# Whole-head rounds in a two-cache decode attention kernel: 64 KB runs, a three-part key ring and one value slot

## The chip, the cores and the metric

One core of one Trainium2 chip. The metric is the device time of one execution in microseconds (us); several executions of each kernel are timed and the median is quoted. The "span" of a profile is the time from the first to the last instruction of one profiled execution. The kernel before takes 1335.8 us.

## The reference

Two attention layers decode one token each. Layer A has 32 heads, each with its own cache of 32,768 keys and values of 128 bf16 numbers (8 MB of keys and 8 MB of values for a head). Layer B has 8 key/value heads for 32 query heads and looks only at the last 4096 positions. In shortened form:

```python
def _A_ref(x, k_cache, v_cache, wq, wo):           # B has rep = 4 and a window of 4096 keys
    q = (x @ wq).reshape(B, Sq, H, Dh).transpose(0, 2, 1, 3)
    scores = jnp.einsum("bhqd,bhkd->bhqk", q, k_cache) * (Dh ** -0.5)
    p = softmax(scores, axis=-1)
    o = jnp.einsum("bhqk,bhkd->bhqd", p, v_cache)
    return o.transpose(0, 2, 1, 3).reshape(B, Sq, H * Dh) @ wo
return jnp.concatenate([a, b], axis=-1)
```

Every key and value is read once: 570.43 MB in all. Nearly all of it is A's cache.

## The kernel before

The program is a list of operations on each engine; dependencies become semaphore waits. DMA requests are made by SP (SyncE), in one order, and wait there until their buffer is free. Keys lie in two buffers of 32 KB per partition, values in two more. A round is half the keys of two heads: two 4 MB pieces of keys (one of each head), two of values. Shortened:

```python
def load_kv(self, which, name, g, r, u):           # one 4 MB piece: 32 KB runs on 128 partitions
    ...
    src = d[which][0, h0:h0 + d["kvu"], base:base + d["blk"], :].rearrange("s (p j) d -> p s (j d)", p=128)
    self.load_slot(which, slot, dst, src)          # waits until this slot is free

for i in range(self.NIT):                          # the main loop, 32 rounds
    g, r = divmod(i, a["R"])
    self.emit_qcopy(g)
    for u in range(2):
        self.load_kv("k", "A", g, r, u)
        self.emit_unit("A", g, r, u)               # T: transpose keys on PE, copy on DVE; S: scores
    self.emit_stats("A", g, r)                     # maximum and exp, running over r
    self.emit_PT("A", g, r)                        # transpose the probabilities
    for u in range(2):
        self.load_kv("v", "A", g, r, u)
        self.emit_PV("A", g, r, u)                 # 128 matmuls of 128 columns for each u
    self.emit_gather("A", g, r)
```

In what follows T is the transposes of the keys (PE into `psT`, DVE copies to `kt`), S the scores into `psS`, PV the product with the values into `psACC`, gather the small matmul into `psG`. Each operation signals one other engine. PV signals DVE, so SP learns that a value buffer is free from the next PE operation, the gather.

## Time and profile before

| | before |
|---|---|
| time, median (range) | 1335.74 us (1335.54 to 1335.80) |
| bytes read, mean rate | 570.43 MB, 428 GB/s |
| one round | 38.86 us for 16.8 MB, 431.8 GB/s |
| PE busy | 956.5 us, 72% |

The page of the kernel before: span, moved GB/s in 40 equal slices, packets, and the chain of waits that ended last (share of the span by line).

```profile
span 1334.2 us, 41413 instructions
...
PE 956.5 (72%) x19416; PEld 771.4 (58%) x19416; DVE 790.9 (59%) x1662; ACT 61.2 (5%) x201; POOL 2.0 (0%) x15
...
GB/s 393 394 424 436 427 435 428 434 430 432 431 433 431 432 431 430 433 431 432 431 432 430 432 433 430 433 431 433 428 434 429 432 432 432 432 430 434 430 433 351
DMA packets 22003, 570.64 MB, mean 428 GB/s; under 512 B 2530, under 2 KB 2532, under 8 KB 2788
...
DMA kbuf<-in_A_k_cache_dram 63%; PE psT L469 23%; PE psS L492 4%; DMA kbuf<-in_A_wo_dram 2%; PE psPT L634 0%; DVE out_sb L638 0%; SPq L291 0%
```

From the ninth slice on the rate is level at 428 to 434 GB/s, but for the last slice. The Trainium skill, "DMA: Bandwidth & Descriptors", section "Where 436 GB/s comes from", gives 435.2 GB/s as the ceiling of the 16 ports through which the DMA engines reach SBUF (the core's own memory), and a lower one, about 358, for loads from HBM (the main memory); this trace goes past the lower one and its level part sits about 1% under 435.2. The DMA queue is the bottleneck, so a question about time is a question about bytes per us and about empty moments.

One round in the timeline of the kernel before (start, length, engine, line, operation; in brackets the idle time ahead of it and what ended it):

```profile
659.86 5.37 PE L469 MATMUL psT<-ident,kbuf 128*128 128x128 bf16 x64 [4.02 <-DMA kbuf<-in_A_k_cache_dram]
...
670.49 10.08 SPq L291 DMA_DIRECT2D kbuf<-in_A_k_cache_dram  x2
...
686.97 3.58 PE L562 MATMUL psACC<-vbuf,ptsb 128*2 128x128 bf16 x128 [0.69 <-ACT ptsb L540]
...
691.09 1.96 PE L562 MATMUL psACC<-vbuf,ptsb 128*2 128x128 bf16 x128 [0.53 <-DVE oc_A L591]
...
693.66 0.44 PE L605 MATMUL psG<-oc_A,hw 128*32 128x1 f32 x4 [0.62 <-DVE oc_A L591]
693.89 0.81 SPq L291 DMA_DIRECT2D vbuf<-in_A_v_cache_dram  x2
```

The next round's T starts at 698.73, 38.87 us later, again after a wait for keys. T starts when the first 4 MB piece has landed, so at 693.89, where the values are asked for, the second piece is still ahead of them in the queue. That is 4.8 us to the landing plus 9.7 us for the second piece.

Four stretches of the table of windows of the kernel before. Columns: stretch, length, busy us of PE, PEld, DVE, ACT and POOL with counts, then the granted clock of PE, the DMA share and GB/s.

```profile
687.00:690.50 3.50, 3.50 (x128) 3.27 (x128) 0.00 (x0) 0.14 (x2) 0.00 (x0) 0.50 1.00 431
691.10:693.10 2.00, 1.94 (x128) 1.75 (x128) 0.00 (x0) 0.00 (x0) 0.00 (x0) 1.00 0.99 426
40.00:44.00 4.00, 3.42 (x40) 2.75 (x44) 4.00 (x7) 1.05 (x4) 0.00 (x0) 0.76 0.85 354
52.00:56.00 4.00, 4.00 (x63) 1.83 (x64) 1.51 (x6) 0.00 (x0) 0.00 (x0) 0.57 0.43 135
```

A hole is a time in which DMA engines have nothing to move.

### The profile page before, as it was taken

What the parts mean: (1) busy time and instruction counts of PE and PEld (TensorE: products, weight loads), DVE (VectorE), ACT (ScalarE), POOL (GpSimd) and SP (SyncE); (2) the same over time, 40 slices, a digit from 0 to 9 for tenths busy, and PEclk for the clock granted to TensorE, in tenths of its full rate; (3) what the DMA queues carried; (4) which work ended last, traced back from release to release, by engine and by line L of the source; (5) the groups of instructions that cost most, each with busy time, mean ns of one, the idle gap of its engine ahead of it and who ended that gap; (6) DMA issues with size and microseconds to landing.
All of it is one profiled execution on the core that took longest, in us unless ns stands there. A gap on an engine that the chain in (4) does not pass through costs nothing.

```text
span 1334.2 us, 41413 instructions
## 1 busy us (share of the span) xinstructions
PE 956.5 (72%) x19416; PEld 771.4 (58%) x19416; DVE 790.9 (59%) x1662; ACT 61.2 (5%) x201; POOL 2.0 (0%) x15
## 2 busy tenths in 40 slices
PE   3677667877767677776668777667777767677776
PEld 3456555656655565665556556555666655566663
DVE  3665555666555566655556665556666555566752
ACT  0000000000000000000000000000000000000000
POOL 0000000000000000000000000000000000000000
PEclk9787878888878888887888898878888878888988
DMA  9999999999999999999999999999999999999998
GB/s 393 394 424 436 427 435 428 434 430 432 431 433 431 432 431 430 433 431 432 431 432 430 432 433 430 433 431 433 428 434 429 432 432 432 432 430 434 430 433 351
DMA packets 22003, 570.64 MB, mean 428 GB/s; under 512 B 2530, under 2 KB 2532, under 8 KB 2788
## 3 DMA queue, kind: packets, MB, share of 16 engines
q1 hardware_dynamic: 21700, 570.44, 99.6%
q8 instruction: 10, 0.16, 0.0%
q10 hardware_dynamic: 288, 0.00, 0.0%
q14 instruction: 5, 0.04, 0.0%
HBM read 570.43 MB, written 0.00 MB: 428 GB/s over the span
## 4 chain that ended last, share of the span: by engine, by line
DMA 65%; PE 26%; issue 0%; DVE 0%; SPq 0%
DMA kbuf<-in_A_k_cache_dram 63%; PE psT L469 23%; PE psS L492 4%; DMA kbuf<-in_A_wo_dram 2%; PE psPT L634 0%; DVE out_sb L638 0%; SPq L291 0%
## 5 line engine op out<-in xcount | busy, mean ns | idle before, releaser
L472 DVE COPY kt<-psT 128x1024 bf16<-128x1024 bf16 x1056 | 655.1, 684 | 214.0 <-PE psT L469 211.6
L469 PE MATMUL psT<-ident,kbuf 128*128 128x128 bf16 x8448 | 576.0, 233 | 139.8 <-DMA kbuf<-in_A_k_cache_dram 129.7
L469 PEld LDWEIGHTS psT<-ident,kbuf 128*128 128x128 bf16 x8448 | 536.0, 106 | 232.8 <-DMA kbuf<-in_A_k_cache_dram 137.8
L562 PE MATMUL psACC<-vbuf,ptsb 128*2 128x128 bf16 (+1 forms) x8256 | 188.4, 271 | 45.4 <-ACT ptsb L540 22.0
L562 PEld LDWEIGHTS psACC<-vbuf,ptsb 128*2 128x2 bf16 (+1 forms) x8256 | 169.2, 106 | 66.8 <-ACT ptsb L540 30.5
L492 PE MATMUL psS<-kt,qw 128*32 128x512 bf16 x2048 | 157.7, 385 | 15.2 <-DVE kt L472 15.2
L537 PE MATMUL psPT<-ident,psb 128*128 128x128 bf16 x136 | 20.7, 307 | 130.9 <-ACT psb L524 130.9
L591 DVE SCALAR_TENSOR_TENSOR oc_A<-psACC,hot_A,oc_A 128x128 f32<-128x128 f32 x48 | 16.8, 351 | 145.5 <-PE psACC L562 145.5
L537 PEld LDWEIGHTS psPT<-ident,psb 128*128 128x128 bf16 x136 | 11.8, 131 | 140.7 <-ACT psb L524 140.3
L524 ACT ACTIVATE psb<-psS,nb_A 128x512 bf16<-128x512 f32 x32 | 22.0, 688 | 1173.9 <-DVE nb_A L523 1173.9
L492 PEld LDWEIGHTS psS<-kt,qw 128*32 128x32 bf16 x2048 | 33.9, 95 | 57.7 <-DVE kt L472 31.0
L588 DVE TENSOR_SCALAR oc_A<-psACC,hot_A 128x128 f32<-128x128 f32 x16 | 5.6, 350 | 92.8 <-PE psACC L562 92.8
L510 DVE TENSOR_REDUCE tr_in<-psS 128x1 f32<-128x512 f32 x34 | 23.5, 692 | 18.4 <-PE psS L492 18.4
L605 PE MATMUL psG<-oc_A,hw 128*32 128x128 f32 (+1 forms) x128 | 14.4, 223 | 23.8 <-DVE oc_A L591 19.4
L513 DVE COPY m<-tr_a 1x16 f32<-1x16 f32 (+1 forms) x136 | 22.3, 164 | 2.6
L605 PEld LDWEIGHTS psG<-oc_A,hw 128*32 128x32 f32 x128 | 6.6, 110 | 28.8 <-issue 28.8
L519 DVE COPY b_A<-mr_A 1x16 f32<-1x16 f32 x128 | 21.2, 165 | 2.4
L540 ACT ACTIVATE ptsb<-psPT 128x512 bf16<-128x512 bf16 x34 | 20.3, 597 | 21.3 <-PE psPT L537 21.3
L574 DVE TENSOR_SCALAR oc_A<-oc_A,alpha_A 128x129 f32<-128x129 f32 x16 | 4.6, 289 | 16.5 <-ACT alpha_A L527 16.5
L426 PE MATMUL psACC<-x_B,vbuf 128*128 128x1 bf16 x128 | 3.6, 165 | 13.5 <-DMA vbuf<-in_B_wq_dram 13.5
L426 PEld LDWEIGHTS psACC<-x_B,vbuf 128*128 128x128 bf16 x128 | 3.5, 104 | 13.4 <-issue 13.4
L527 ACT ACTIVATE alpha_A<-cm_A,nb_A 128x1 f32<-128x1 f32 x32 | 9.0, 282 | 0.0
(71 smaller groups left out, 107.6 us busy)
## 6 DMA issues: line engine op xcount, KB each, us to landing
kbuf<-in_A_k_cache_dram SPq DMA_DIRECT2D x64, 4096.0 KB, 28.2
vbuf<-in_A_v_cache_dram SPq DMA_DIRECT2D x64, 4096.0 KB, 30.6
kbuf<-in_B_k_cache_dram SPq DMA_DIRECT2D x2, 4096.0 KB, 27.8
vbuf<-in_B_v_cache_dram SPq DMA_DIRECT2D x2, 4096.0 KB, 18.6
vbuf<-in_B_wq_dram SPq DMA_DIRECT2D x1, 4096.0 KB, 12.6
vbuf<-in_A_wq_dram SPq DMA_DIRECT2D x1, 4096.0 KB, 41.8
kbuf<-in_B_wo_dram SPq DMA_DIRECT2D x2, 2048.0 KB, 25.9
kbuf<-in_A_wo_dram SPq DMA_DIRECT2D x1, 1536.0 KB, 22.5
```

Source lines behind the costliest of these rows:

```text
L469: inst = e.transpose(T[:, 128 * k:128 * k + 128], src[:, DH * tile:DH * tile + DH], self.ident[:, :])
L472: self.copies.append(self.op("dve", lambda v: v.tensor_copy(KT[:, :], T[:, :]), o, to="pe"))
L492: inst = e.matmul(self.S[32 * c:32 * c + 32, :], lhsT=win, rhs=self.kt[(bb + c // 2) % NKT][:, 512 * (c % 2):512 * (c % 2) + 512], start=f ...
L510: o = dve(lambda v: v.reduce_max(tr["in"][:, 0:1], self.S[:, :], axis=AXX), self.sdone, self.k_pool)
L513: x = dve(lambda v, c=c: v.tensor_copy(m4[0:1, W * c:W * c + W], tr["a"][32 * c:32 * c + 1, 0:W]), o)
L519: x = dve(lambda v, c=c: v.tensor_copy(t["b"][32 * c:32 * c + 1, 0:W].rearrange("p (k h) -> p k h", k=KC), t["mr"][0:1, k, :].unsqueeze(1) ...
L524: self.sread = self.op("act", lambda s: s.activation(out=self.psb[:, :], in_=self.S[:, :], func=ACTF.Exp, bias=t["nb"][:, k:k + 1], scale= ...
L537: inst = e.transpose(PT[:, 128 * jj:128 * jj + 128], self.psb[:, 128 * jj:128 * jj + 128], self.ident[:, :])
L540: self.ptread = self.op("act", lambda s: s.activation(out=self.ptsb[:, :], in_=PT[:, 0:512], func=ACTF.Copy), self.psread, to="pe")
L562: inst = e.matmul(acc[32 * c:32 * c + HG, 0:w], lhsT=pt[:, col:col + HG], rhs=vv[:, :, 16 * kc + 4 * c + jj, :], start=(kc == 0 and jj == ...
L591: self.oop = dve(lambda v, src=src, hot=hot: v.scalar_tensor_tensor(out=oc, in0=src, scalar=hot, in1=oc, op0=ALU.mult, op1=ALU.add), pv, b ...
L605: self.gath = self.op("pe", lambda e, c=c, c2=c2: e.matmul(self.G[0:32, c0 + c:c0 + c2], lhsT=win, rhs=t["oc"][:, c:c2], start=False, stop ...
```

## The change

A round becomes one whole head. Its 8 MB of keys are one transfer with 64 KB runs per partition into two neighbouring thirds of a 96 KB ring, its 8 MB of values one transfer into a single 64 KB slot. There is then no running maximum and no rescaling, and PV uses 64 matmuls of 512 columns. The intent is fewer, longer runs and less compute. The middle third is used by every head and transposed first, so that the next head's keys can be asked for half way through T. The last head's keys still come in two pieces. The startup is reordered as well.

```diff
-        self.kbuf = [sb(f"kbuf{i}", [128, UT * DH], BF16) for i in range(2)]
-        self.vbuf = [sb(f"vbuf{i}", [128, UT * DH], BF16) for i in range(2)]
+        self.kbuf = sb("kbuf", [128, 3 * HALF * DH], BF16)
+        self.vbuf = sb("vbuf", [128, 2 * HALF * DH], BF16)
 ...
+    def k_thirds(self, g):
+        return (1, 0) if g % 2 == 0 else (1, 2)
+    def load_k(self, g, parts):
 ...
+        if parts == 1:
+            self.load(self.kbuf[:, w * lo:w * lo + 2 * w], src, self.mark("k", 0), *free)
+            sem = self.mark("k", 1)
+            self.op("sp", lambda e: e.sem_inc(sem, 16))
+        else:
+            for i, t in enumerate(self.k_thirds(g)):
+                self.load(self.kbuf[:, w * t:w * t + w], src[:, w * (t - lo):w * (t - lo) + w], self.mark("k", i), *free)
+    def load_v(self, g):
+        self.load(self.vbuf[:, :], self.kv_src("v", "A", g)[:, 0, :], self.mark("v", 0), *self.free["v"])
 ...
         self.load_wq("B")
-        for g in range(2):
-            self.load_kv("k", "B", g, 0, 0)
+        self.load_b("k", 0)
         self.load_wq("A")
+        self.load_b("k", 1)
         self.emit_qproj("B")
-        self.emit_unit("B", 0, 0, 0)
+        self.emit_unit("B", 0)
+        self.emit_qproj("A")
 ...
-        for i in range(self.NIT):
-            g, r = divmod(i, a["R"])
-            self.loop = {"pe": i, "dve": g}
+        for g in range(NQH):
+            self.loop = {"pe": g // 2, "dve": g // 2}
+            self.load_k(g, 1 if g < NQH - 1 else 2)
+            self.load_v(g)
 ...
+            todo = [(c, pt[:, :, 32 * c + kc], self.vbuf[:, DH * (16 * kc + 4 * c):DH * (16 * kc + 4 * c + 4)], kc == 0, kc == 15)
+                    for kc in range(16) for c in range(STRIPS)]
 ...
+        pv = self.op("pe", mm, self.landed("v", 0 if name == "A" else g), self.ptread, self.accread, to="dve")
+        for i in (0, 1) if name == "A" else (g,):
+            self.free["v"][i] = pv
```

## The prediction

> **What bounds it now.** Data transfers. The page's slices show DMA at 9 tenths throughout, 430 to 434 GB/s in most; queue q1 holds 99.6%. In the timeline a round (half the keys of two heads, 16.8 MB) repeats every 38.86 us: 431.8 GB/s. PE works about 28 us of it (table of windows) and waits 129.7 us in all for keys (list of waits), so PE has slack; the chain of waits is 63% key loads. The Trainium skill, "DMA: Bandwidth & Descriptors", section "Where 436 GB/s comes from", puts the ceiling at 435.2 GB/s; the trace agrees, no long stretch is above it. The page's 570.43 MB at that rate is an estimated 1311 us, 1.9% below today: over 2% is practically out of reach.
>
> **What the change does.**
> 1. Runs double. In the trace's packet records 32 KB take 1.214 to 1.218 us, 16 KB 0.611 to 0.615, 8 KB 0.309 to 0.316, 4 KB 0.160: a line with 9 to 13 ns fixed per packet. If a 64 KB run is one packet, head loads need 512 fewer on each engine: 5 to 6 us saved (estimate from these); a round becomes about 38.7 us.
> 2. Startup. Before, one value load and A's first keys are issued only at 53.7 us (timeline); DMA is at 0.85 in 40 to 44 us and 0.43 in 52 to 56 (table of windows), about 2.8 us lost. Now A's projection runs earlier, the second value half is asked for near 40 us: 2.5 to 3 us gained.
> 3. Compute. PV becomes 64 matmuls of 512 columns instead of 256 of 128; rescaling, running maximum and alpha go. PV took 6.1 us with its gap (timeline); I expect 4. Off the critical path.
> 4. Queue depth. Next keys go out when the middle third is transposed, 10.6 us into the round, while values (19.4 us) are moving. Values go out at the gather, about 32.8 us in, 6 us before the keys in flight land. A transfer takes about 2.5 us to start (the hole at 53.7), so the queue should stay full, with 3.5 us to spare instead of about 12.
> 5. Tail. The last values land as one 8 MB piece; the last PV starts about 2 us later, and the end comes about 1 us later.
>
> Sum: -5.5 - 2.7 + 1 = about -7 us.
>
> **Prediction: 1328.7 us**, 8 in 10 between 1323.5 and 1335. Chances: faster by over 2% 0.02, within 2% 0.95, slower by over 2% 0.03.
>
> **What would show the steps right or wrong.** About 14,000 packets rather than 22,003, the 64 KB ones taking 2.42 us (1; if packets stay at 32 KB, only 2 us are gained in all). DMA share near 1 between 40 and 60 us (2). PE busy down by some 60 us (3). Value issues 5 to 6 us before keys land, steady slices at 432 to 434 GB/s (4). The last PV about 29 us after the last head's first keys (5).
>
> **What would make it wrong.** Value slot freed too late under a low granted clock: a hole of 1 to 2 us each round, +30 to +60 us. PE's loop over two heads is about 1560 instructions (780 matmuls, each with its weight load) against 1170; the skill's "Runtime: NRT & Kernel Launch", section "Instruction fetch mechanics", gives PE room for 2048, in blocks of 256. Today instruction fetches stop after the first rounds; if the longer loop refetches, stalls like the 4.5 us one at 110 us recur and use up the spare of step 4. 64 KB runs could stream slower from memory than 32 KB ones; nothing in this trace shows it.

## The result

The changed kernel takes 1341.97 us (1340.55 to 1344.51, 4 runs) beside 1335.77 (1335.54 to 1336.15) for the kernel before. Ratios are computed as the mean time of one kernel's runs over that of the other's of the same rounds, so they are not quite the ratio of the medians: here 1.0048, 95% interval 1.0031 to 1.0066. I had predicted a gain of 7 us with a range of 1323.5 to 1335; it lost 6.

The page of the changed kernel:

```profile
span 1340.9 us, 28815 instructions
...
PE 960.0 (72%) x13272; PEld 667.2 (50%) x13272; DVE 804.6 (60%) x1660; ACT 54.8 (4%) x167; POOL 2.0 (0%) x15
...
GB/s 395 442 427 428 422 426 438 432 420 428 436 409 438 438 409 438 438 434 432 416 436 434 411 438 426 420 438 438 432 428 422 438 438 438 438 432 420 427 439 284
DMA packets 12932, 570.66 MB, mean 426 GB/s; under 512 B 1522, under 2 KB 1524, under 8 KB 1780
```

Many slices read 438 and others 409, but slices cannot be read so finely here: a slice is 33.5 us long and a packet is booked whole at its start, so 14 packets of 64 KB on each of 16 engines make 438 GB/s and 13 make 407. What the page does show is the mean, 426 against 428, and a last slice of 284 against 351. PE busy has not fallen.

A round in the timeline of the changed kernel, and the end of the next one:

```profile
670.18 5.57 PE L485 MATMUL psT<-ident,kbuf 128*128 128x128 bf16 x64 [3.05 <-DMA kbuf<-in_A_k_cache_dram]
...
681.00 0.33 SPq L283 DMA_DIRECT2D kbuf<-in_A_k_cache_dram  x1
...
697.31 5.60 PE L573 MATMUL psACC<-vbuf,ptsb 128*4 128x512 bf16 x64 [0.69 <-ACT ptsb L548]
...
704.62 0.44 PE L599 MATMUL psG<-oc_A,hw 128*32 128x1 f32 x4 [1.72 <-DVE oc_A L587]
704.85 0.33 SPq L283 DMA_DIRECT2D vbuf<-in_A_v_cache_dram  x1
...
709.71 6.25 PE L485 MATMUL psT<-ident,kbuf 128*128 128x128 bf16 x64 [4.65 <-DMA kbuf<-in_A_k_cache_dram]
...
737.51 5.97 PE L573 MATMUL psACC<-vbuf,ptsb 128*4 128x512 bf16 x64 [0.69 <-ACT ptsb L548]
...
745.42 0.33 SPq L283 DMA_DIRECT2D vbuf<-in_A_v_cache_dram  x1
...
748.41 5.70 PE L485 MATMUL psT<-ident,kbuf 128*128 128x128 bf16 x64 [2.77 <-DMA kbuf<-in_A_k_cache_dram]
```

PV starts 27.1 us after T starts, as before, and takes 5.60 us, not 4. The values are asked for 34.7 us into the round, not 32.8, and 4.9 us before the next T. In the next round PV takes 5.97 us, and the request comes 35.7 us into the round, only 3.0 us before the next T. Now all 8 MB of keys have to land before T starts, so nothing stands behind these keys in the queue when they land.

Windows of the changed kernel (columns as before): the two parts of this PV, and the stretch where the startup hole was.

```profile
697.31:701.20 3.89, 3.89 (x40) 1.31 (x44) 0.00 (x0) 0.15 (x2) 0.00 (x0) 0.50 1.17 505
701.20:702.90 1.70, 1.70 (x32) 0.50 (x24) 0.00 (x0) 0.00 (x0) 0.00 (x0) 0.96 1.07 463
52.00:56.00 4.00, 4.00 (x71) 2.99 (x68) 4.00 (x8) 0.00 (x0) 0.00 (x0) 1.00 1.00 416
```

The startup hole is closed (DMA share 1.00 against 0.43). PV runs its first 3.9 us at half clock. (For the booking of packets named above, the DMA share of a short window can pass 1.)

The trace's packet records say more. I chained each packet to the one whose end it follows, which gives 16 series, one per engine. Then I summed, between 100 and 1280 us, the gaps of more than 50 ns between packets ("gaps"), and what packets that took more than 1.02 times their usual length took beyond the usual length ("slow packets"), both in us as means over 16 engines. "Holes" counts value requests in the steady part followed within 8 us by more than 0.2 us of such loss. "Lead" is the median time from the request of the values to the next T, "pair" the median length of two rounds, "end" the time from the last input byte to the end of the span. These are one profiled execution each; "again" is the same changed kernel on another chip.

| kernel | span | gaps | slow packets | holes | lead | pair | end |
|---|---|---|---|---|---|---|---|
| before | 1334.2 | 0.3 | 0.2 | 0 of 29 | 4.75 (+9.7 queued) | 77.73 | 4.1 |
| changed | 1340.9 | 3.1 | 7.7 | 10 of 28 | 4.04 | 77.75 | 8.6 |
| again | 1336.3 | 2.6 | 5.5 | 8 of 29 | 4.08 | 77.62 | 6.8 |
| early | 1332.5 | 1.0 | 2.1 | 2 of 29 | 5.79 | 77.41 | 6.8 |
| late | 1349.0 | 8.0 | 11.5 | 14 of 28 | 2.87 | 78.56 | 9.2 |
| later | 1356.2 | 15.1 | 11.4 | 16 of 28 | 1.70 | 78.85 | 8.4 |
| khalves | 1331.6 | 0.3 | 0.2 | 0 of 29 | | | 5.7 |
| same32 | 1348.1 | 2.9 | 8.7 | 14 of 28 | 4.24 | 78.15 | 11.1 |
| earlytail | 1330.7 | 0.8 | 2.6 | 4 of 29 | 5.42 | 77.41 | 5.4 |
| earlytail32 | 1334.8 | 0.8 | 1.6 | 1 of 29 | 5.52 | 77.72 | 5.9 |
| tail | 1338.0 | 4.7 | 7.7 | 9 of 28 | 3.92 | 77.81 | 4.2 |

In the changed kernel a 64 KB run is one packet: 8064 packets of 65,536 bytes, median 2.418 us; without holes two rounds take 77.4 us. So the faster packets are there. What ate them is in the columns gaps, slow packets and end.

### The profile page after: what moved, and what is told of

It reads as the page before. It is cut to its first block, busy times and chain, and to the rows that moved or that the text cites. A ratio compares the mean times of both kernels' runs of the same rounds, so it can differ in the third digit from the quotient of the medians. Undisturbed runs are those within 1.5% of the kernel's fastest.

```text
span 1340.9 us, 28815 instructions
## 1 busy us (share of the span) xinstructions
PE 960.0 (72%) x13272; PEld 667.2 (50%) x13272; DVE 804.6 (60%) x1660; ACT 54.8 (4%) x167; POOL 2.0 (0%) x15
## 4 chain that ended last, share of the span: by engine, by line
DMA 68%; PE 28%; DVE 3%; issue 0%; ACT 0%; SPq 0%
DMA kbuf<-in_A_k_cache_dram 65%; PE psT L485 23%; PE psS L507 3%; DMA kbuf<-in_B_k_cache_dram 3%; DVE kt L488 3%; PE psACC L573 1%; PE psS L629 1%; PE psPT L629 1%; DVE oc_A L587 0%; ACT psb L535 0%; PE psPT L545 0%; DVE tr_in L524 0%; DVE b_A L530 0%; SPq L283 0%; DVE m L527 0%
## 5 line engine op out<-in xcount | busy, mean ns | idle before, releaser
L573 PE MATMUL psACC<-vbuf,ptsb 128*4 128x512 bf16 (+1 forms) x2112 | 189.2, 536 | 23.3 <-ACT ptsb L548 22.0
L507 PE MATMUL psS<-kt,qw 128*32 128x512 bf16 x2048 | 157.6, 385 | 15.5 <-DVE kt L488 15.5
L585 DVE TENSOR_SCALAR oc_A<-psACC,hot_A 128x128 f32<-128x128 f32 x32 | 11.2, 351 | 254.8 <-PE psACC L573 254.8
L573 PEld LDWEIGHTS psACC<-vbuf,ptsb 128*4 128x4 bf16 (+1 forms) x2112 | 61.0, 112 | 142.7 <-issue 95.6
L545 PEld LDWEIGHTS psPT<-ident,psb 128*128 128x128 bf16 x136 | 11.5, 128 | 137.5 <-ACT psb L535 137.3
L587 DVE SCALAR_TENSOR_TENSOR oc_A<-psACC,hot_A,oc_A 128x128 f32<-128x128 f32 x96 | 33.7, 351 | 3.4
L629 PE MATMUL psS<-kbuf,oz_B 128*1 128x512 bf16 x32 | 8.4, 428 | 0.0
L525 DVE STREAM_TRANSPOSE tr_a<-tr_in 128x32 f32<-128x32 f32 x34 | 7.2, 212 | 1.2
```

Of the source, the lines that this page charges most:

```text
L507: inst = e.matmul(self.S[32 * c:32 * c + 32, :], lhsT=win, rhs=self.kt[(bb + c // 2) % NKT][:, 512 * (c % 2):512 * (c % 2) + 512], start=b ...
L545: inst = e.transpose(PT[:, 128 * jj:128 * jj + 128], self.psb[:, 128 * jj:128 * jj + 128], self.ident[:, :])
L573: inst = e.matmul(acc[32 * c:32 * c + rows, 0:512], lhsT=lhsT, rhs=rhs, start=begin, stop=end, tile_position=(0, 32 * c), skip_group_check ...
L587: o = self.op("dve", lambda v, src=src, hot=hot: v.scalar_tensor_tensor(out=oc, in0=src, scalar=hot, in1=oc, op0=ALU.mult, op1=ALU.add), p ...
L629: inst = e.matmul(bank[0:1, 0:512], lhsT=t["oz"][:, a:a + 1], rhs=wo[:, 512 * a:512 * a + 512], start=(a == 0), stop=(a == 31), skip_group ...
```

## The experiments

Three theories. Q (queue): the values are asked for too late, engines that finish their share of the keys early run dry, and a restart costs a gap and a slow first packet. P (packets): 64 KB packets stream worse by themselves, in bursts. Theory T (tail; not the transposes T): the last two heads' compute starts only when whole heads of keys have landed, so the end comes late. In the texts the packet clock was set 0.6 to 1.1 us wrong; "7.7" and "3.5 us" from last byte to end are 8.6 and 4.1 in the table, and "2.7 us to start" is about 1.0 us to the first packet, see below.

### early: the value slot is reported free right after PV

```diff
-        for i in (0, 1) if name == "A" else (g,):
-            self.free["v"][i] = pv
+        done = pv
+        if name == "A":
+            PT = self.PT[:, :].bitcast(BF16)
+            done = self.op("pe", lambda e: e.transpose(PT[:, 512:640], self.ident[:, :], self.ident[:, :]), to="sp")
+        for i in (0, 1) if name == "A" else (g,):
+            self.free["v"][i] = done
```

The added transpose writes an unused part of PSUM, the memory of matmul results; its only use is the signal, which follows PV on the same engine.

> The changed kernel (median 1342 us) with one thing moved: the signal that the value slot is free is given by a small PE transpose right after the PV matmuls, not by the gather 1.7 us later. Theory Q (the value request comes too late: 3.5 to 4.2 us before the keys in flight have landed, a transfer needs about 2.7 us to start, and the engines that finish the keys first run dry): the slow first packets at the value issues go, about 8 to 11 us less, 1331 to 1334 us; steady rounds of 38.7 us without gaps. Theory P (64 KB packets stream worse by themselves, in bursts): slow packets stay, within 2 us of 1342. The tail of 9 us after the last input byte stays in both.

Measured: 1335.19 us (1333.37 to 1336.78), 6.8 less than the changed kernel's median (5.7 less than in the control run told below), ratio to before 0.9996 (0.9982 to 1.0009). From its timeline:

```profile
655.39 5.95 PE L573 MATMUL psACC<-vbuf,ptsb 128*4 128x512 bf16 x64 [0.69 <-ACT ptsb L548]
...
661.27 0.23 PE L580 MATMUL psPT<-ident 128*128 128x128 bf16 x1
...
661.53 0.33 SPq L283 DMA_DIRECT2D vbuf<-in_A_v_cache_dram  x1
...
666.32 5.37 PE L485 MATMUL psT<-ident,kbuf 128*128 128x128 bf16 x64 [2.83 <-DMA kbuf<-in_A_k_cache_dram]
```

The request follows PV by 0.2 us. The lead grows by 1.75 us, holes fall from 10 of 28 to 2 of 29, with every packet still 64 KB. That is Q; P had said within 2 us of 1342. The gain is under the 8 to 11 us that I expected, and two holes are left.

The packet records let Q be counted request by request. In the traces of changed, again, early, late and later I took all 151 value requests between 100 and 1280 us, and the moment when the first engine ended its share of the keys. In 52 cases that was before the request or at most 1.1 us after it (about what a middle engine takes from the request to its first packet), and in 51 of them a hole followed. In the other 99 cases there were 3 holes. At 745.42 above, the first engine ended 0.56 us after the request, and the hole cost 0.98 us; at 704.85 it ended 2.33 us after, and there was none.

### late and later: the same signal held back

```diff
+            if name == "A" and to is None:
+                first = self.gath
+        if name == "A":
+            for n in range(2):                      # later: range(4)
+                first = self.op("act", lambda s: s.activation(out=self.idle[:, :], in_=self.psb[:, :], func=ACTF.Copy), first)
+            self.free["v"] = [first, first]
```

> The opposite: the value slot is reported free only after two extra ScalarE copies that follow the gather, about 1.3 us later than in the changed kernel. Theory Q: each hole delays the keys two rounds on, so about half of the added 1.3 us appears in every round: 31 x 0.65 = some 20 us more, 1355 to 1370 us, holes at almost every value issue. Theory P: within 3 us of 1342.

> Four ScalarE copies instead of the two of the late run ahead of the signal for the value slot, so another 1.2 to 1.3 us later. The late run lost 10 us where I had expected 20. If the loop that paces the kernel spans two rounds (values of a head cannot start before the head two back is done, so two rounds share one delay) and late had first to use up what was left of the spare, the full half now shows: 30 x 0.6 = 18 to 20 us more than late, 1369 to 1373 us. If each round paid the whole delay: 37 us more, 1387 to 1392. If the loss is only the restart of the engines (a fixed cost for each hole): less than 5 us more.

From late's timeline, the gather, the two copies, the request and the next T:

```profile
708.90 0.44 PE L600 MATMUL psG<-oc_A,hw 128*32 128x1 f32 x4 [1.72 <-DVE oc_A L588]
709.13 1.29 ACT L607 ACTIVATE idle<-psb 128x512 bf16<-128x512 bf16 x2 [7.95 <-PE psG L600]
710.44 0.33 SPq L284 DMA_DIRECT2D vbuf<-in_A_v_cache_dram  x1
711.81 5.89 PE L486 MATMUL psT<-ident,kbuf 128*128 128x128 bf16 x64 [2.47 <-DMA kbuf<-in_A_k_cache_dram]
```

Measured: late 1352.31 us (1350.84 to 1353.44), 10 more than the changed kernel; later 1357.53 us (1357.10 to 1357.88), 5 more again. Gather to request is 1.55 us in late and 2.87 in later. Direction and order are those of Q, and P (within 3 us) is refuted. Both sizes were wrong. For late I had taken the spare to be gone already in every round, but only every third request found it gone. For later the request came only 0.7 us later after T (36.5 to 37.2 us), because in that trace PV started 0.4 us earlier after T and was 0.2 us shorter (medians 27.06 and 5.57 us against 27.46 and 5.78), and a hole opens at about every second request only. The gaps do grow with the delay (3.1, 8.0, 15.1), while the slow first packets stop growing (7.7, 11.5, 11.4). The 5.2 us more lie just beside the third case, a fixed cost for each hole (under 5 us), but gaps that grow are not a fixed cost. The rest of the shortfall stays open.

### khalves: keys of every head in two pieces

```diff
-            self.load_k(g, 1 if g < NQH - 1 else 2)
+            self.load_k(g, 2)
-        self.ksem = [s(f"ksem{i}") for i in range(2)]
+        self.ksem = [s(f"ksem{i}") for i in range(3)]
-                ... self.mark("k", i), *free)
+                ... self.mark("k", t), *free)
```

A semaphore for each third is needed: with two, pieces of two heads would be in flight on one semaphore.

> The changed kernel, but the keys of every head come as two 4 MB pieces of 32 KB runs, each with its own semaphore (one per third of the ring), so transposes start after the first half has landed; values stay one 8 MB piece of 64 KB runs in one slot. Theory Q: compute runs 9.7 us further ahead of the queue, values are requested some 13 us before the queue runs out, no holes; half of the packet gain is left (2.7 us) and the tail of before comes back: 1329 to 1332 us. Theory P: value packets are still 64 KB, so about half of the slow packets stay (5 us): 1334 to 1337.

Measured: 1333.84 us (1333.35 to 1336.04), 2 us above what Q said and at the border of what P said; by time alone inconclusive. The trace decides: the values are still 64 KB packets, yet there is no hole (0 of 29) and slow packets add 0.2 us. So 64 KB packets are not slow by themselves. The reason for the missing 2 us is not settled; its end, 5.7 us, is longer than the 4.1 of before.

### same32: only the packet size undone

```diff
-            self.load(self.kbuf[:, w * lo:w * lo + 2 * w], src, self.mark("k", 0), *free)
+            for t in self.k_thirds(g):
+                self.load(self.kbuf[:, w * t:w * t + w], src[:, w * (t - lo):w * (t - lo) + w], self.mark("k", 1), *free)
-        self.load(self.vbuf[:, :], self.kv_src("v", "A", g)[:, 0, :], self.mark("v", 0), *self.free["v"])
+        for i in range(2):
+            self.load(self.vbuf[:, w * i:w * i + w], src[:, w * i:w * i + w], self.mark("v", i), *self.free["v"])
```

T waits for both key pieces and PV for both value pieces.

> The changed kernel with nothing but the packet size undone: keys and values of a head are still requested at the same moments and waited for as a whole (8 MB each), but each as two transfers of 32 KB runs. Theory Q: the holes stay and the fixed cost per packet comes back (5.5 us): 1345 to 1350 us. Theory P: the bursts go (about -10) and the fixed cost comes back (+5.5): 1336 to 1339 us.

Measured: 1350.82 us (1347.83 to 1352.17), 0.8 above the range of Q and 12 above that of P. Holes at 14 of 28 requests with 32 KB packets: the holes belong to the waits, not to the packet size. P is refuted.

### tail and earlytail: the last two heads' keys in halves

```diff
-            self.load_k(g, 1 if g < NQH - 1 else 2)
+            self.load_k(g, 1 if g < NQH - 2 else 2)
```

with the semaphore per third of khalves; earlytail adds the early signal.

> The changed kernel, but the keys of the last two heads (before: of the last head only) come as two 4 MB pieces of 32 KB runs, with their own semaphores, so that the transposes of the second to last head start 9.7 us earlier. Theory T (the end is late because the last two heads' compute, two rounds of about 35 us plus the projections, starts only when the whole 8 MB of keys of the second to last head has landed): the time from the last input byte to the end falls from 7.7 us to about the 3.5 us of before, 1337.5 to 1339 us. Rival (the end is late only because the holes have delayed the data): the 7.7 us stay, within 1.5 us of 1342.

> Both repairs in one: the early signal for the value slot and the last two heads' keys in halves. In the early run 5.7 us pass from the last input byte to the end; with 3.5 it would be 2 us less than that run's 1335.2: 1332.5 to 1334 us, which is also 2 to 3 us under the kernel before. If only the holes mattered, no change from 1335.2.

First the end of the changed kernel and of tail in their timelines (PE alone). Changed:

```profile
1288.72 3.82 PE L485 MATMUL psT<-ident,kbuf 128*128 128x128 bf16 x64
...
1314.35 5.98 PE L573 MATMUL psACC<-vbuf,ptsb 128*4 128x512 bf16 x64 [0.69 <-ACT ptsb L548]
...
1331.52 7.07 PE L629 MATMUL psPT<-kbuf,oz_A 128*1 128x512 bf16 x32
```

Tail:

```profile
1286.03 3.82 PE L485 MATMUL psT<-ident,kbuf 128*128 128x128 bf16 x64
...
1313.61 5.07 PE L573 MATMUL psACC<-vbuf,ptsb 128*4 128x512 bf16 x64 [2.63 <-DMA vbuf<-in_A_v_cache_dram]
...
1328.64 7.07 PE L629 MATMUL psPT<-kbuf,oz_A 128*1 128x512 bf16 x32
```

In the changed kernel the last head's T starts at 1288.72 without any wait for keys and its PV waits for the softmax: PE is behind the data. In tail PV waits 2.63 us for values: PE is ahead again, and the end follows the last byte by 4.2 us instead of 8.6. Measured times: tail 1340.01 us (1337.96 to 1342.46), only 2 less than the changed kernel and 0.9 less than the control (which ran on another chip): between what theory T and its rival had said, and not separated by the spread. Without the holes it shows: earlytail 1331.67 us (1331.00 to 1332.46) against early's 1335.19, and the two ranges do not overlap (the two ran on different chips, but the kernel before took 1335.88 and 1335.86 us beside them). Of these 3.5 us, the profiled ends account for 1.5 (6.8 to 5.4 us); the rest is not explained. Earlytail was expected at 1332.5 to 1334 and beat that. Its ratio to the kernel before is 0.9968 (0.9955 to 0.9982): it beats both kernels, by 4.2 us the one before and by 10 the changed one.

### bstart: the new startup order alone, in the kernel before

```diff
-        for g in range(2):
-            self.load_kv("k", "B", g, 0, 0)
+        self.load_kv("k", "B", 0, 0, 0)
         self.load_wq("A")
+        self.load_kv("k", "B", 1, 0, 0)
 ...
         self.emit_unit("B", 0, 0, 0)
+        self.emit_qproj("A")
         self.emit_stats("B", 0, 0)
```

(the hook that made A's projection later is removed)

> The kernel before with nothing but the order of the start of the change: wq of A before the second B keys, and A's projection after the first B unit. If the start is worth what the two traces say (2.0 us at 24 to 60 MB moved), 1333.3 to 1334.5 us; if the start gains nothing by itself, 1335.5 to 1336.3.

Measured: 1334.10 us (1333.84 to 1334.21), 1.8 less than before beside it. In its trace 24 MB have arrived 2.8 us earlier than before, as in the changed kernel (2.9).

### earlytail32 and again: the packet size without holes, and a control

The first is earlytail with the loads of same32; the second is the changed kernel unchanged.

> Both repairs (early signal, last two heads' keys in halves), but all loads of heads split into 32 KB runs while still requested and awaited as a whole. With hardly any holes in either, the difference from the run with 64 KB runs (1331.7 us) is the packet size alone: my estimate of the fixed cost per packet says 5.2 us (30 heads of 32 packets fewer on each engine, 10 to 11 ns each), 1336 to 1338 us, and a clean pair of rounds of 77.7 us instead of 77.4. If the packet size is worth nothing, 1331 to 1333.

> The changed kernel unchanged, on this chip, as a control: 1340 to 1344 us; its last input byte and its end 7 to 8 us apart. A median under 1338 would mean that part of the differences so far is between chips or sessions.

Measured: earlytail32 1339.18 us (1336.32 to 1340.89), 7.5 more than earlytail and 1.2 above the range that I had given. The pair of rounds is 77.72 against 77.41 us, which is 15.5 x 0.31 = 4.8 us over the run, close to my 5.2; the two profiled spans differ by 4.1. The other 2 to 3 us of the timed difference are open; the two runs were on different chips. The control gave 1340.90 us (1338.04 to 1341.67), ratio 1.0038 (1.0024 to 1.0052): it reproduces.

## Why the prediction was wrong

1. **Longer runs: right.** One packet of 64 KB, 2.418 us, against two of 1.214 to 1.218. Two rounds without a hole take 77.4 us against 77.73, 5 us over the run; I had said 5 to 6.
2. **Startup: right.** The hole is gone, 2.0 to 2.9 us earlier in the trace, 1.8 us alone in timed runs, somewhat under the 2.5 to 3 that I had said.
3. **Compute: wrong.** "PV took 6.1 us with its gap (timeline); I expect 4", and "PE busy down by some 60 us". PV took 5.3 to 6.1 us and PE busy rose from 956.5 to 960.0. I divided the work by the mean granted clock (0.85). The clock record shows 0.50 for the first 3.5 to 5.1 us of PV (median 4.3). The Trainium skill, "TensorE: Matmul & The Clock Gate", section "What's actually happening", says that the clock falls to half after an idle window of about 3.4 us. PE waits 4.0 us for the softmax just before PV, and in each of the 30 steady rounds the clock fell 1.9 to 3.5 us into that wait: as the page says in kind, though mostly sooner than after 3.4 idle us. A group of four 512-column matmuls starts every 0.43 us at that clock. The same 0.50 was visible in the trace of before.
4. **Queue depth: this is the step that failed.** "Values go out at the gather, about 32.8 us in, 6 us before the keys in flight land ... so the queue should stay full, with 3.5 us to spare". They went out about 35.0 us in, with a median lead of 4.0 us and leads down to 2.7. Of the 2.2 us, 1.7 are the error of step 3, a PV of 5.7 us (median) for 4: PV was not "off the critical path", because the request waits for its end. I also left out that the 16 engines do not finish together: in the changed kernel their ends of one key transfer spread over 0.6 to 3.3 us (median 1.5). The estimate from the traces: 4.0, less about 0.4 us from the last byte to T, less about 1.0 us from a request to its first packet, leaves 2.6 us, and 1.3 at the shortest lead, against that spread. (The 2.5 us that I had subtracted were the time to nearly the full rate in the startup hole; its first packet began 1.0 us after the request.) So some requests are in time and others not. Gaps and slow restarts cost 10.8 us in the profiled run and 8.1 in the control, against 0.5 before. Early (earlier signal: 6.8 us back), late and later (held back: 10 and 16 lost), khalves (no holes with 64 KB values) and same32 (holes with 32 KB packets) show that the lead is the cause and the packet size is not. What I had listed first under "What would make it wrong" is this hole, but with 1 to 2 us in each round; it came to 0.2 to 1.1 us in one round of three.
5. **Tail: right in direction, the term mis-sized.** "The end comes about 1 us later"; from the last byte to the end it was 2.7 to 4.5 us more. I placed the last T at the landing of the last head's first key half. But by then PE was still busy with the head before, whose T could start only when its whole 8 MB had landed. The end of tail's trace (4.2 us) and the times of earlytail show it; tail's time alone does not.

In sum for the profiled run, in us: startup -2.3 (the difference once the start is over), packets -5, holes +10.3, end +4.5, together +7.5; the spans differ by +6.7. The fear that the longer PE loop would refetch its instructions was unfounded: fetches of 16 KB stop at about 148 us, before the second pass of the loop begins, but for one at the end.

## What to carry to other kernels

When transfers are merged, count what stands in the queue behind the last piece at the moment the next request is made, in the slowest round and for the engine that finishes first, not on average: here 10 us of queued work were traded for 5 us of faster packets. Free a buffer by a signal of its own right after the last read, not by the next convenient operation. Near the end, where no further data hide the compute, go back to small pieces, and take the length of a block on PE from the clock granted in that block.

## What the Trainium skill lacked or had wrong

- "DMA: Bandwidth & Descriptors" does not say what a 64 KB run saves over two of 32 KB: here it is one packet of 2.418 us, against 1.2135 us for 32 KB, so about 9 ns are fixed for each packet even at this size.
- The same page gives about 0.6 us to the first byte of a request from SP (section "Latency and other measured facts"). It does not say from which moment it counts: in late and later, where the queue was dry, the first packet began 0.95 to 0.97 us after the start of the issuing instruction (33 requests), which takes 0.33 us, so about 0.63 us after its end. Counted from the end, the trace agrees.
- No page says how far apart the engines of one transfer end: here, between the first and the last, 0.6 to 3.3 us in the changed kernel, 1.5 to 3.3 in early and 0.4 to 2.0 in late. Nor does one say that the first packets after a dry moment are slow: 64 KB packets of mostly 2.8 to 3.3 us instead of 2.4.
- "Runtime: NRT & Kernel Launch", section "Instruction fetch mechanics", calls the instruction memory both 128 KiB for PE and only two blocks of 16 KiB. The runs fit the first: a PE loop of some 1560 instructions (780 matmuls with their weight loads) ran 16 times with no fetch of 16 KB after the first pass until its end.
